# V stores of 8 or 16 tokens per segment, reordered by token and then segment, and without the number that the kernel's own scheduler held for them

## The chip, the cores and the metric

One core of one Trainium2 chip. The metric is the device time of the whole program in microseconds (us), the median of several runs. A run's granted clock is the mean share of full speed that TensorE was given; every run here had 0.989 to 1.000, and none was put in the slow state. Comparisons of kernels are ratios: the mean time of one kernel's runs over that of the other's runs of the same rounds on the same chip, so not quite the ratio of the medians that are quoted beside them.

## The reference

A memory-augmented attention layer and a gated feed-forward (FFN), both twice, on 2048 tokens of width 512. Attention runs over 64 segments of 32 tokens; 8 memory tokens, which are the output of the segment before, are put in front of each.

```python
for s in range(n_seg):
    h = jnp.concatenate([mem, xs], axis=1)          # 8 memory tokens + 32 tokens
    q, k, v = (einsum('btd,dhe->bhte', h, W) for W in (Wq, Wk, Wv))   # 32 heads of 128
    p = softmax(where(mask, einsum('bhqe,bhke->bhqk', q, k) * scale, -1e9))
    o = einsum('bhte,hed->btd', einsum('bhqk,bhke->bhqe', p, v), Wo)
    mem = o[:, :8]; outs.append(o[:, 8:])
...
x = x + A(layernorm(x)); x = x + B(layernorm(x))    # twice
```

The V rows of these 32 tokens don't depend on the memory. The kernel computes those of 24 of them ahead of time, for whole blocks of 4 segments, and parks them in HBM.

## The kernel before

`take_v` copies the normalised, transposed tokens of a block (4 segments, `BLK`) into columns of a weight tile of 128 columns; 24 tokens per segment fill 96 columns, and the last 32 are filled with 8 tokens per segment of another block (a "fill"). `v_pass` multiplies the tile with Wv in 8 column blocks of 512, copies each result to a staging tile and stores it to the HBM scratch `scr`, whose rows run by segment, then token.

```python
def take_v(self, pst, B, j, tile, keys, c0, r0, n):
    off = r0 + (MEM if j else 0)
    dst = fview(tile[:, 0, c0:c0 + 1], [(P, self.DC), (n, BLK), (1, n)])
    self.pl.add(("ACT", "DVE"), copy_ns(16 * n, True),
                lambda: (dst, fview(pst()[:, 0, off:off + 1], [(P, self.DC), (SEG, BLK), (1, n)])), r=[B], w=keys)

def v_pass(self, tile, keys, pieces, boot=False):
    ...                       # cut: matmuls and the copy to the staging tile vs
    for c0, j, b, r0, n in pieces:
        d = self.scr[j][b * BLK * XS:(b + 1) * BLK * XS, ps].rearrange("(i r) e -> i r e", i=BLK)[:, r0:r0 + n, :]
        tk = pl.add(("SP", "POOL") if boot else "SP", ..., lambda ...: ("dma", d, vs[c0:c0 + BLK * n, 0:512 * w]), ...)
        if n == 8:
            tk.land = 8000.0
```

Nothing is issued there. Every operation is a task with an expected duration; a list scheduler (`Planner`) plays the whole program through on a model of the engines, up to 24 rounds, keeps the round with the shortest model time, and the program is then written in that order. `land` is how long the model lets an SP transfer hold one of eight lanes:

```python
        if e == "SP":
            lanes.append(end + tk.land)          # 3000 ns unless set
            if len(lanes) >= 8:
                free[e] = max(end, lanes[-8])
```

## Time and profile before

| | before |
|---|---|
| time, median of 3 runs | 1872.28 us (1869.12 to 1873.32) |
| TensorE (PE) busy | 1822.6 us, 97% |
| chain that ended last | PE 92%, DMA 0% |
| 96 KB V stores (full blocks, 128 of them) | 16 semaphore updates, 1.82 us from issue to landing (median) |
| 32 KB V stores (fills, 96 of them) | 5 semaphore updates, 2.12 us |

The prediction below shows the lines. Landing times of SP transfers are not on the page; here and below they are counted from the updates of a transfer's semaphore in the trace.

### The profile page before, as it was taken

Reading aid. Unit: us, or ns where it says so; the run is one execution under the profiler, and the core shown is the slowest. Engines: PE = TensorE matmul, PEld = TensorE weight load, DVE = VectorE, ACT = ScalarE, POOL = GpSimd, SP = SyncE. Lnnn points to the kernel's source line nnn. Section 1 sums busy time; section 2 is a strip of 40 time slices with the busy share of each in tenths; the row PEclk is TensorE's granted clock in tenths of the full one; section 3 lists DMA queues with packets and bytes.
Section 4 is the critical chain, followed back from the end, with each engine's and each line's share of the span. In section 5 each row is a group of like instructions: output and inputs, shape, how many; then the busy total and the mean of one; then the engine's idle time right before and its main releaser. Section 6 shows DMA issues by size and latency. Waiting matters only on the chain.

```text
span 1869.7 us, 94235 instructions
## 1 busy us (share of the span) xinstructions
PE 1822.6 (97%) x41068; PEld 1577.4 (84%) x41282; DVE 1282.3 (69%) x4167; ACT 1137.3 (61%) x2692; POOL 583.2 (31%) x832
## 2 busy tenths in 40 slices
PE   7999999999999999999999999999999999999999
PEld 3578788888989898989988898989889898988787
DVE  5366577776777667776677677666777677766565
ACT  4655556666666666566666666666666666666554
POOL 5412012332423232333323233233323232333323
PEclk9999999999999999999999999999999999999999
DMA  9733334554645544555545554555545454455534
GB/s 354 247 102 103 89 86 119 153 155 129 182 124 153 151 143 124 151 151 149 166 128 152 147 143 131 141 152 153 157 121 152 136 156 122 141 152 145 158 100 138
DMA packets 130060, 273.83 MB, mean 146 GB/s; under 512 B 29254, under 2 KB 60750, under 8 KB 129646
## 3 DMA queue, kind: packets, MB, share of 16 engines
q0 software_dynamic: 59984, 184.49, 33.7%
q1 hardware_dynamic: 69662, 83.30, 15.5%
q8 instruction: 323, 5.29, 1.2%
q14 instruction: 91, 0.75, 0.1%
HBM read 221.85 MB, written 27.26 MB: 133 GB/s over the span
## 4 chain that ended last, share of the span: by engine, by line
PE 92%; DVE 4%; ACT 2%; issue 1%; DMA 0%; POOL 0%; SPq 0%; ACTq 0%; DVEq 0%; POOLq 0%
PE bank L708 32%; PE bank L811 16%; PE bank L910 11%; PE bank L570 9%; PE bank L680 7%; PE bank L722 5%; PE bank L781 4%; PE bank L794 4%; PE bank L934 4%; PE bank L540 1%; DVE st L735 1%; ACT otsb L1002 1%; DVE pb L764 0%; DMA vsb<-sst 0%; PE bank L878 0%
## 5 line engine op out<-in xcount | busy, mean ns | idle before, releaser
L708 PE MATMUL bank<-hT,wq_sb 128*128 128x80 bf16 (+1 forms) x8960 | 624.2, 198 | 5.7 <-issue 1.7
L708 PE MATMUL bank<-hT,wk_sb 128*128 128x80 bf16 (+1 forms) x8960 | 622.9, 198 | 1.4 <-issue 1.4
L1002 ACT CAST qku<-bank 128x480 bf16<-128x480 f32 (+3 forms) x770 | 393.9, 512 | 265.5 <-PE bank L708 253.3
L708 PEld LDWEIGHTS <-wq_sb 128*128 128x128 bf16 x8960 | 458.1, 99 | 27.9 <-issue 8.5
L708 PEld LDWEIGHTS <-wk_sb 128*128 128x128 bf16 x8960 | 450.7, 99 | 1.6 <-issue 1.6
L735 DVE TENSOR_TENSOR st<-bank,maskb 80x240 f32<-80x240 f32 (+1 forms) x732 | 268.7, 368 | 234.5 <-PE bank L722 227.7
L811 PE MATMUL bank<-otsb,wo_sb 128*128 128x80 bf16 (+1 forms) x8960 | 371.8, 198 | 7.4 <-ACT otsb L1002 5.5
L811 PEld LDWEIGHTS <-wo_sb 128*128 128x128 bf16 x8960 | 339.7, 99 | 21.5 <-issue 10.3
L902 POOL DMA_DIRECT2D wg<-in_B_w_gate_dram x217 | 165.0, 760 | 489.4 <-PE bank L910 419.7
L1002 ACT CAST otsb<-bank 128x480 bf16<-128x480 f32 (+3 forms) x420 | 200.8, 486 | 76.7 <-PE bank L794 61.9
L928 POOL DMA_DIRECT2D wd<-in_B_w_down_dram x217 | 153.7, 710 | 256.6 <-PE bank L794 98.5
L764 DVE TENSOR_TENSOR pb<-st,rz 80x480 bf16<-80x480 f32 x348 | 205.8, 592 | 3.5
L745 ACT ACTIVATE st<-st 80x240 f32<-80x240 f32 (+3 forms) x420 | 159.8, 382 | 64.6 <-DVE st L742 62.7
L1002 ACT CAST ptsb<-bank 128x480 bf16<-128x480 f32 (+3 forms) x315 | 155.3, 499 | 65.2 <-PE bank L781 62.9
L530 POOL TENSOR_TENSOR lns<-lns,negh 128x1 f32<-128x1 f32 (+1 forms) x79 | 45.4, 576 | 449.0 <-DVE lns L529 334.7
L722 PE MATMUL bank<-qku 128*80 128x80 bf16 (+1 forms) x2240 | 176.7, 202 | 1.8 <-ACT qku L1002 0.4
L747 DVE TENSOR_REDUCE sm<-st 80x6 f32<-80x240 f32 (+3 forms) x420 | 151.7, 362 | 35.5 <-ACT st L745 33.4
L910 PE MATMUL bank<-xnT,wg 128*128 128x128 bf16 (+2 forms) x1784 | 171.8, 219 | 1.5 <-ACT xnT L1002 0.2
L910 PE MATMUL bank<-xnT,wu 128*128 128x128 bf16 (+2 forms) x1784 | 171.2, 218 | 0.1
L722 PEld LDWEIGHTS <-qku 128*80 128x80 bf16 (+1 forms) x2240 | 129.9, 117 | 46.2 <-issue 11.5
L903 POOL DMA_DIRECT2D wu<-in_B_w_up_dram x217 | 162.5, 749 | 4.6 <-PE bank L781 1.4
L742 DVE TENSOR_TENSOR st<-st,mx 80x240 f32<-80x240 f32 (+3 forms) x420 | 155.7, 371 | 3.9
(98 smaller groups left out, 2475.1 us busy)
## 6 DMA issues: line engine op xcount, KB each, us to landing
wg<-in_B_w_gate_dram POOLq DMA_DIRECT2D x220, 256.0 KB, 4.3
wu<-in_B_w_up_dram POOLq DMA_DIRECT2D x220, 256.0 KB, 4.7
wd<-in_B_w_down_dram POOLq DMA_DIRECT2D x220, 256.0 KB, 5.2
vsb<-scr SPq DMA_DIRECT2D x508, 48.0 KB
vsb<-sst SPq DMA_DIRECT2D x280, 64.0 KB
scr<-vst SPq DMA_DIRECT2D x128, 96.0 KB
wv_sb<-in_A_Wv_dram SPq DMA_DIRECT2D x4, 1024.0 KB
wq_sb<-in_A_Wq_dram SPq DMA_DIRECT2D x5, 768.0 KB
```

Of the source, the lines that this page charges most:

```text
L570: nc.tensor.matmul(B[:, :], lhsT=tile[:, c, :], rhs=self.wv[:, c, cs], start=(c == 0), stop=(c == DC - 1))
L708: nc.tensor.matmul(o_ap, lhsT=W[:, c, h * P:(h + 1) * P], rhs=mv(c), start=(c == 0), stop=(c == DC - 1))
L722: nc.tensor.matmul(s_all(SB)[pr, uh - h0 + i, :], lhsT=qku[:, i, 0, 0:ncol], rhs=qku[:, i, 1, 0:ncol], start=True, stop=True)
L735: pl.add("DVE", dve_ns(n, True), lambda gsz=gsz, hs=hs, st=st, SB=SB, pj_=pj_, npj_=npj_, mk=mk, idx=idx: nc.vector.tensor_tensor(out=st[p ...
L742: pl.add("DVE", dve_ns(n), lambda gsz=gsz, hs=hs, st=st, mx=mx: nc.vector.tensor_tensor(out=st[pr, hs], in0=st[pr, hs], in1=mx[pr, hs].uns ...
L745: pl.add("ACT", act_ns(n), lambda hs=hs, st=st: nc.scalar.activation(out=st[pr, hs], in_=st[pr, hs], func=ACTF.Exp, scale=self.scale), r=s ...
L764: nc.vector.tensor_tensor(out=o, in0=st[pr, hs].unsqueeze(1).to_broadcast([npart, 2, gsz, L]), in1=rz[pr, :, 0:gsz].unsqueeze(3).to_broadc ...
L811: nc.tensor.matmul(WB[:, c * ncol:(c + 1) * ncol], lhsT=self.wo[:, h, c * P:(c + 1) * P], rhs=otsb[:, hl, 0:ncol], start=(h == 0 and c == ...
L902: pl.add("POOL", 760, lambda wg=wg, fs=fs: nc.gpsimd.dma_start(out=wg[:], in_=self.wgv[:, :, fs]), r=[("wo", self.H - 1)], w=[gk] + bt, la ...
L903: pl.add("POOL", 760, lambda wu=wu, fs=fs: nc.gpsimd.dma_start(out=wu[:], in_=self.wuv[:, :, fs]), r=[("wo", self.H - 1)], w=[uk] + bt, la ...
L910: nc.tensor.matmul(gu[:, 2 * i + k, 0:n], lhsT=W[:, c, i * P:(i + 1) * P], rhs=xnT[:, c, rw], start=(c == 0), stop=(c == DC - 1))
L1002: nc.scalar.copy(out=dst, in_=src)
```

## The change

The intent: the outermost dimension of these stores is 4; ordered by token and then segment it is 8 or 16, and such a store was expected to land sooner. With the slow store gone, the line that tells the scheduler of it goes too. Stores of 24 tokens per segment, which are contiguous, stay as they are.

```diff
-        dst = fview(tile[:, 0, c0:c0 + 1], [(P, self.DC), (n, BLK), (1, n)])
+        dst = fview(tile[:, 0, c0:c0 + 1], [(P, self.DC)] + ([(n, BLK), (1, n)] if n == XS else [(1, BLK), (BLK, n)]))
 ...
-                d = self.scr[j][b * BLK * XS:(b + 1) * BLK * XS, ps].rearrange("(i r) e -> i r e", i=BLK)[:, r0:r0 + n, :]
-                tk = pl.add(("SP", "POOL") if boot else "SP", ...
+                d = self.scr[j][b * BLK * XS:(b + 1) * BLK * XS, ps]
+                if n < XS:
+                    d = d.rearrange("(i r) e -> r i e", i=BLK)[r0:r0 + n]
+                pl.add(("SP", "POOL") if boot else "SP", ...
 ...
-                if n == 8:
-                    tk.land = 8000.0
```

So the edit has four parts that can be taken apart: the fills' stores, the stores of the start, the copies that now write with a stride, and the number.

More of the change, by code (lines that the diff above doesn't have):

```diff
@@ L580, in v_pass @@
             for c0, j, b, r0, n in pieces:
-                d = self.scr[j][b * BLK * XS:(b + 1) * BLK * XS, ps].rearrange("(i r) e -> i r e", i=BLK)[:, r0:r0 + n, :]
-                tk = pl.add(("SP", "POOL") if boot else "SP", {"SP": 450, "POOL": 760} if boot else 450,
+                d = self.scr[j][b * BLK * XS:(b + 1) * BLK * XS, ps]
+                if n < XS:
+                    d = d.rearrange("(i r) e -> r i e", i=BLK)[r0:r0 + n]
+                pl.add(("SP", "POOL") if boot else "SP", {"SP": 450, "POOL": 760} if boot else 450,
                        lambda vs=vs, d=d, c0=c0, n=n: ("dma", d, vs[c0:c0 + BLK * n, 0:512 * w]), lat=3000.0 + 1500.0 * boot,
```

## The prediction

> **What bounds the kernel now.** I read the page from the top: first the busy shares, then the chain that ended last.
>
> ```profile
> PE 1822.6 (97%) x41068; PEld 1577.4 (84%) x41282; DVE 1282.3 (69%) x4167; ACT 1137.3 (61%) x2692; POOL 583.2 (31%) x832
> ...
> q0 software_dynamic: 59984, 184.49, 33.7%
> q1 hardware_dynamic: 69662, 83.30, 15.5%
> ...
> PE 92%; DVE 4%; ACT 2%; issue 1%; DMA 0%; POOL 0%; SPq 0%; ACTq 0%; DVEq 0%; POOLq 0%
> ```
>
> TensorE (PE) is busy 1822.6 of 1869.7 us, so it is idle for 47.1 us in all. The weight loads cover 84%. The queue in which the V stores run after the start, q1 (the one that SyncE, SP, issues to), takes 15.5% of the DMA engines' time. The chain is PE for 92% and DMA for 0%. The kernel is bound by TensorE; a transfer counts only where TensorE stands still for it.
>
> Next the waits of PE, which say what its idle time was spent on, and of its weight loads:
>
> ```profile
> PE bank L513 <- DVE ident L451: 6.4, 1, 6.4
> PE bank L811 <- ACT otsb L1002: 5.5, 19, 0.7
> PE bank L540 <- DVE xn L531: 4.8, 5, 2.8
> PE bank L708 <- issue: 3.1, 5, 1.1
> PE bank L781 <- DVE pb L764: 2.3, 6, 1.0
> PE bank L794 <- DMA vsb<-sst: 1.5, 3, 0.9
> ```
>
> Columns are total us, times, longest. One row names a DMA: 1.5 us, for vsb<-sst, not for the stores at issue. From windows of 20 us I see where the rest lies: 0 to 20 us holds 10.7 us of idle (20.00 less 9.28), the last 9.7 us hold 3.2, 120 to 260 us hold 7.7; from 440 us on most windows have PE busy 19.6 to 19.9 of 20.
>
> Then the stores. The profile lists them as scr<-vst, 128 of 96 KB and 96 of 32 KB:
>
> ```profile
> scr<-vst SPq DMA_DIRECT2D x128, 96.0 KB
> ...
> scr<-vst SPq DMA_DIRECT2D x96, 32.0 KB
> ```
>
> The 96 small ones are the 8-token pieces ("fill" pieces: 4 fills x 3 pieces x 8 column blocks), all between 208 and 1379 us. Pieces of 16 tokens exist only in the start (before about 130 us), issued mostly from GpSimd (POOL). The waits of SP's queue and the view of the tile vst show who depends on them:
>
> ```profile
> SPq L668 <- PE bank L794: 441.9, 206, 6.6
> SPq L689 <- DVE sst L1004: 386.9, 55, 13.0
> ...
> SPq L668 <- DMA scr<-vst: 21.3, 18, 2.7
> ```
>
> ```profile
> who waited for it (us, times):
>   DVE st L735: 0.7, 1
> ```
>
> SP's queue waits 21.3 us in 18 places for a V store to land. It waits twenty times as long for TensorE (441.9 us for buffers that PV matmuls read), so it normally has slack. Of all engines only VectorE ever waited on the staging tiles vst, 0.7 us.
>
> **The size of the cost, from the trace's semaphore updates.** For each SP DMA I took the updates of its semaphore from issue to the next use of that semaphore. The 32 KB stores show 5 updates, the 96 KB ones 16, the 24-row loads vsb<-scr 13. Median time from issue to the last update: 2.12 us for 32 KB, 1.82 us for 96 KB. Issuing itself took 0.62 us against 0.31 us. Less issue, that is 1.50 against 1.51 us: the small store is slow in its issue[...]. 76 of the 96 landed within 2.45 us; 20 took 3 to 6.8 us, in the second half of a pass[...]. Their excess over 2.12 us sums to 49 us.
>
> [...]
>
> **The change part by part.**
>
> 1. Store shape. [...] What of it reaches TensorE: at most the row of 1.5 us and the matching row of weight loads (0.8 us). 0 to -2 us.
>
> 2. Boot stores. 24 pieces of 8 tokens and 24 of 16, nearly all from GpSimd, where 16 updates were seen for every shape and landing took 5 to 7 us whatever the shape (96-row ones too: 5.9 us). TensorE is busy 19.73 us of 20 in 20 to 80 us. 0 to -1 us.
>
> 3. The copies take_v. 24 of them now write 2-byte elements 8 bytes apart. On ScalarE the copies run at 0.83 ns an element (128, 256, 384 elements: 265, 376, 480 ns), a rate that should not care. On VectorE 225, 292, 358 ns is 0.52 ns an element; strided it might fall to 1.04, by my choice of the worst case, so 67 ns more for 128 elements. Three copies sat there. Under 0.5 us, and not on the chain.
>
> 4. The removed line `tk.land = 8000`. This is the part that can move something. The order of all instructions comes from a list scheduler in the kernel's build, and this number is how long it thinks an 8-token store holds one of SP's eight lanes. The trace's 2.12 us says that 3000 is the truer number. Did it matter in the plan? In 205.7 to 228.7 us SP issued 31 DMAs: 1.35 per us. Eight lanes at 3 us carry 2.7 per us. With a quarter of them at 8 us the mean is 4.25 us and they carry 1.9 per us; near the limit only in bursts. So in the old plan SP was sometimes held in a fill pass; in the new one it isn't, stores and loads move by some us, and from there the greedy choices and the best of 24 rounds may differ all the way down. The amount of work stays the same: same matmuls, same copies. What can differ is TensorE's idle time outside start and end, about 33 us (47.1 - 10.7 - 3.2), and slack within busy time. I take a change of a quarter of that either way, 8 us, as the typical size.
>
> Sum: direct -1 (0 to -3), plan 0 with a spread of 8. 1872.3 - 1 is about 1871; I lean slightly lower, since a truer model should on average not hurt: 1870.
>
> **The rivals.**
>
> - The slow stores were really holding back the loads behind them, and the V passes get faster as a whole. For it: the chain of waits passes once through scr<-vst near 211 us (1.69 us) and through vsb<-sst near 214.5 us (2.10 us), and fill passes at 200 to 220 us show PE busy only 18.03 of 20. Against: that stretch's idle is named DVE pb and ACT otsb as well, and DMA waits of PE add up to 2.3 us in the whole run. Even if every one of 12 fill passes gained 1 us: 1860.
> - The new order is worse: the plan was tuned with 8000, and the freed SP queue may bring vsb<-scr loads or stores earlier, against the FFN weight loads (queue q0, 33.7%), or put softmax work in a worse order. Speaking for it: 8% of the chain, some 150 us, runs through other engines. Against: all PE waits on such work are under 1 us but for three or so. It would make 1878 to 1885.
> - The transfers are hidden anyway and the plan hardly moves: 1870 to 1874, within the spread of the three runs (1869.12 to 1873.32). I think this the likeliest.
> - Strided writes or the new DRAM order slow the copies or the store: each run stays 1 KB (2 KB in the start), so no smaller pieces; copies are hidden. 0 to +2.
>
> **Range and chances.** Noise is 4 us from lowest to highest run; the plan's spread of 8 dominates. 8 in 10: 1861 to 1880. Over 2% is 37 us either way. Faster by that would need most of TensorE's 47 us idle gone, of which 14 lie at start and end: 2%. Slower by that needs nearly double the idle: 2%. Within: 96%.
>
> **What would show it.** In the changed trace: 32 KB stores with 9 updates[...], landing near 2.0 us with issue still about 0.6; fewer beyond 3 us; PE's busy time within 10 us of 1822.6 and its share of the chain at 90% or more; SP's wait for scr<-vst below 21.3 us without a gain in span; 96 KB stores unchanged at 1.8. The prediction is wrong if PE's idle time outside start and end moves by over 15 us: then the plan, not the stores, is the cause, and restoring the 8000 would tell.

Step 1's 0 to -2 us comes from the measured waits of 1.5 and 0.8 us of TensorE and its weight loads, and the sum came to -1 us on 1872.3, about 1871, put at 1870.

## More of the kernel before

One more line of the kernel before is needed for comparison: the busy times in one stretch, 200 to 1400 us, where all 96 fills lie. Its columns are the stretch, its length, then busy us and instructions of PE, of the weight loads (PEld), of VectorE (DVE), ScalarE (ACT) and GpSimd (POOL), and last the granted clock, the DMA share and GB/s.

```profile
200.00:1400.00 1200.00, 1178.06 (x26518) 1043.82 (x26658) 852.70 (x2779) 750.29 (x1719) 360.62 (x501) 1.00 0.49 140
```

PE shows 21.9 us of idle in these 1200 us.

## The result

The changed kernel took 1873.01 us (median of 4 runs, 1870.35 to 1873.84) beside 1872.53 us: ratio 1.0004, 95% interval 0.9986 to 1.0021. A second measurement on one chip with experiments gave 0.9992 (0.9978 to 1.0005). The predicted 1870 (1861 to 1880) holds it.

The stretch of 200 to 1400 us of the changed kernel:

```profile
200.00:1400.00 1200.00, 1184.69 (x26740) 1051.32 (x26868) 866.16 (x2788) 760.57 (x1734) 366.55 (x501) 1.00 0.49 140
```

PE's idle fell from 21.9 to 15.3 us there. But the whole time did not fall, so it came back elsewhere. The waits of PE (total us, times, longest) name one candidate; SP's wait for the V stores comes after them:

```profile
PE bank L540 <- DVE xn L531: 5.9, 6, 2.8
PE bank L795 <- DMA vsb<-sst: 3.0, 5, 1.3
PE bank L812 <- ACT otsb L1003: 1.9, 5, 0.5
```

```profile
SPq L669 <- DMA scr<-vst: 17.4, 18, 2.7
```

The wait for ScalarE's otsb fell from 5.5 to 1.9 us, that for xn (the normalised tokens) rose from 4.8 to 5.9. SP's wait for the V stores fell from 21.3 to 17.4 us. The fill stores show 9 semaphore updates and land in 1.93 us instead of 2.12, 6 of 96 over 3 us instead of 20; their issue takes 0.66 us instead of 0.62. Two of these signs were foretold, but are not the new shape's doing. Of the fill stores of e1 below (new shape, number kept) 27 took over 3 us, of those of e2 (old shape, number removed) none in one trace and 1 in the other: the late ones went with the number. And SP's wait is 21.3 us in one trace of e2 and 18.1 in the other, so a fall from 21.3 to 17.4 says little. Last, the copies. The groups of instructions of ScalarE, with shapes kept apart, before and then after:

```profile
L1002 ACT COPY xvl<-bank 128x128 bf16<-128x128 bf16 x12 | 2.6, 298 | 0.0
...
L1002 ACT COPY xvf<-bank 128x256 bf16<-128x256 bf16 x5 | 1.7, 376 | 0.9 <-PE bank L570 0.9
L1002 ACT COPY xvf<-bank 128x128 bf16<-128x128 bf16 x4 | 1.1, 265 | 1.4 <-PE bank L570 1.4
```

```profile
L1003 ACT COPY xvl<-bank 128x128 bf16<-128x128 bf16 x12 | 4.3, 542 | 0.0
L1003 ACT COPY xvf<-bank 128x256 bf16<-128x256 bf16 x5 | 3.3, 772 | 0.8 <-PE bank L571 0.8
...
L1003 ACT COPY xvf<-bank 128x128 bf16<-128x128 bf16 x4 | 1.8, 442 | 1.7 <-PE bank L571 1.7
```

The number after the comma is the mean in ns: 256 elements per partition went from 376 to 772, 128 from 265 to 442. The time between the two sizes is now 330 ns for 128 elements, 2.6 ns each, where it was 0.87.

To see where time is lost I used the moment at which each of the 41,282 weight loads starts, which all traces have in full. The changed kernel is 1.0 us behind at load 250 (43 us), 1.4 at load 750, 1.4 at load 3500 (190 us), 4.7 at load 3750 (200 us), and then gains: 1.2 at load 9000, -3.4 at load 36,500. So something delays the start, and something else pays it back.

### The profile page after: what moved, and what is told of

The parts are those of the page before. It is cut to its first block, busy times and chain, and to the rows that moved or that the text cites. A ratio compares the mean times of both kernels' runs of the same rounds, so it can differ in the third digit from the quotient of the medians.

```text
span 1868.6 us, 94264 instructions
## 1 busy us (share of the span) xinstructions
PE 1824.7 (98%) x41085; PEld 1579.3 (85%) x41282; DVE 1294.5 (69%) x4168; ACT 1143.7 (61%) x2691; POOL 586.3 (31%) x832
## 4 chain that ended last, share of the span: by engine, by line
PE 92%; DVE 4%; ACT 2%; issue 1%; DMA 1%; SPq 0%; POOL 0%; ACTq 0%; DVEq 0%
PE bank L709 32%; PE bank L812 16%; PE bank L911 11%; PE bank L571 9%; PE bank L681 7%; PE bank L723 5%; PE bank L935 4%; PE bank L782 4%; PE bank L795 4%; PE bank L540 1%; DVE pb L765 1%; ACT otsb L1003 1%; DVE st L736 0%; DVE lns L527 0%; DVE sm L748 0%
## 5 line engine op out<-in xcount | busy, mean ns | idle before, releaser
L812 PE MATMUL bank<-otsb,wo_sb 128*128 128x80 bf16 (+1 forms) x8960 | 375.8, 198 | 4.1 <-ACT otsb L1003 1.9
L530 POOL TENSOR_TENSOR lns<-lns,negh 128x1 f32<-128x1 f32 (+1 forms) x79 | 51.1, 648 | 502.3 <-DVE lns L529 445.3
L1003 ACT CAST ptsb<-bank 128x480 bf16<-128x480 f32 (+3 forms) x300 | 147.6, 501 | 55.5 <-PE bank L782 54.1
```

Source lines behind the costliest of these rows:

```text
L812: nc.tensor.matmul(WB[:, c * ncol:(c + 1) * ncol], lhsT=self.wo[:, h, c * P:(c + 1) * P], rhs=otsb[:, hl, 0:ncol], start=(h == 0 and c == ...
L1003: nc.scalar.copy(out=dst, in_=src)
```

## The experiments

The theory that I took from this: the stores themselves are hidden; the new plan gains several us; the strided copies and something about the start take them back. The rival: the plan does nothing much, and the gain is what the new stores bring. The experiments run through the parts. In each I compared the instruction order: with 8000 kept, TensorE's order is that of the kernel before, instruction for instruction; with 8000 removed it is that of the changed kernel. All results were reported correct, that of e8 too: see there.

A summary first. "Clock loss" is (1 - granted clock) x span, the mean over a kernel's runs. It is measured (the record rounds the clock to 0.001, which is 1.9 us), but that taking it off gives the time at full clock is an assumption, good where TensorE is the bound.

| kernel | 8000? | stores in the start | fills' stores | copies | ratio to before (95%) | mean us | clock loss us | mean less loss |
|---|---|---|---|---|---|---|---|---|
| before | yes | old | old | plain | 1 | 1873.8, 1872.5, 1872.7 | 5.4, 4.6, 4.9 | 1868.4, 1867.9, 1867.8 |
| after | no | new | new | strided writes | 1.0004, 0.9992 | 1872.6, 1871.0 | 10.3, 8.7 | 1862.3, 1862.3 |
| e1 shape only | yes | new | new | strided writes | 1.0028 (1.0015 to 1.004) | 1879.2 | 7.9 | 1871.4 |
| e5 | yes | new | new | strided reads | 1.0012 (0.9998 to 1.0025) | 1876.4 | 8.2 | 1868.2 |
| e2 number only | no | old | old | plain | 0.9959 (0.9945 to 0.9973), 0.9955 (0.9941 to 0.997) | 1866.3, 1864.3 | 6.3, 5.2 | 1860.0, 1859.1 |
| e3 | no | old | new | strided in fills | 0.9964 (0.9952 to 0.9977) | 1867.4 | 8.2 | 1859.2 |
| e7 | no | new | new | strided reads | 0.9981 (0.9967 to 0.9995) | 1869.0 | 8.4 | 1860.6 |
| e9 | no | new | old | strided reads in the start | 0.9978 (0.9964 to 0.9992) | 1868.5 | 8.2 | 1860.3 |
| e8 copies only | no | old | old | strided writes | 0.9971 (0.9955 to 0.9987) | 1867.6 | 5.9 | 1861.7 |
| e4 stores doubled | yes | old | 192 halves | plain | 1.0001 (0.9989 to 1.0014) | 1872.8 | 4.9 | 1867.9 |

### The two halves of the edit: e1 and e2

e1 is the changed kernel with the number put back; e2 is the kernel before with the number removed.

```diff
 # e1, against after                 # e2, against before
+                if n == 8:          -                if n == 8:
+                    tk.land = 8000.0  -                    tk.land = 8000.0
```

> New store shape and new copies, but the number 8000 kept: TensorE's instruction order is then the same as in the kernel before, instruction for instruction. Theory (transfers are hidden; the store's shape costs nothing that TensorE sees, the slower strided copies cost about 1 us in the start): 1872 to 1875, ratio 0.9995 to 1.002; 32 KB stores with 9 updates landing at 1.93 us instead of 2.12. Rival (slow stores held the V passes back): 1860 to 1868.

> Old store shape and old copies, only the line with 8000 removed: TensorE's order is that of the changed kernel. Theory: the plan alone gains the 2 to 4 us that the changed kernel makes up between 440 and 1860 us, and the start isn't slowed by copies, so 1868 to 1872, ratio 0.997 to 1.000. Rival (the plan does nothing, the shape does it all): equal to before within 0.05%, 1872.5. Stores with 5 updates, landing about 2.12 us.

Measured: e1 1878.92 us (ratio 1.0028), e2 1865.12 us (0.9959; in a repeat 1863.53, 0.9955). Two effects of opposite sign: removing the number gains 8 us, the new shape costs 5 us under the old plan. e1 was slower than I expected, e2 faster. The rival falls on both counts: the stores do not gain (e1 is slower than before, although its stores land in 1.94 us) and the plan is the gain.

> The changed kernel itself, once more, beside the kernel before on one chip. If plan (-0.41% alone) and shape (+0.28% alone) add up, the ratio is near 0.9987, between 0.9970 and 1.0004; if the shape costs more under the new plan, it stays at 1.0004 or above.

The changed kernel again: 0.9992, inside the range of the sum, 0.9987. The halves add up within the noise.

> The land-only kernel once more. Ratio near 0.9959 again, 0.9945 to 0.9975. Also a test of the clock: kernels with the old store shape lost 5.2 us a run to a granted clock below 1 (30 runs, (1 - clock) x span), those with the new shape 8.5 us (36 runs). If that goes with the store shape, this one loses 4 to 6.5; if it goes with the plan, 8 to 10.

The repeat held, ratio and clock loss both (5.2 us).

### The stores made worse: e4

The kernel before, its order kept, each small store issued as two of half the width, which doubles their number, their issue time and the lanes they take.

```diff
+                if ... tk.land == 8000.0 and tk.on == "SP":
+                    for q in range(2):
+                        nc.sync.dma_start(out=got[1][:, :, 256 * q:256 * q + 256], in_=got[2][:, 256 * q:256 * q + 256])
```

> The kernel before with its order kept, each of the 96 small stores issued as two of half the width: [...]0.6 us more of SP's queue each, 8 stores more per pass. Theory (stores are hidden): ratio 1.000, within 0.002, with SP's waits for scr<-vst grown to 30 us or more. Rival (slow fill stores cost what the change set out to gain): each pass loses 1 us or more, ratio 1.006 or above.

The transfers of e4, and SP's wait for them (total us, times, longest):

```profile
scr<-vst SPq DMA_DIRECT2D x128, 96.0 KB
scr<-vst SPq DMA_DIRECT2D x192, 16.0 KB
```

```profile
SPq L668 <- DMA scr<-vst: 11.5, 18, 1.8
```

Ratio 1.0001, interval 0.9989 to 1.0014: doubling these stores costs nothing that these runs can tell (0.14% at most). My side expectation failed: SP's wait for the stores did not grow to 30 us but fell to 11.5, the half stores landing in 1.88 us instead of 2.12. So fill stores are hidden in the kernel before, with room to spare, and an earlier landing could hardly gain anything; e3 below tests the new shape itself.

### The copies: e5, e7 and e8

e5 is e1 with the copies walked the other way, tokens outside and segments inside. The same elements go to the same places, but the writes are contiguous and the reads from PSUM take the stride (64 bytes).

```diff
-  dst: [(P, DC), (1, BLK), (BLK, n)]      src: [(P, DC), (SEG, BLK), (1, n)]
+  dst: [(P, DC), (BLK, n), (1, BLK)]      src: [(P, DC), (1, n), (SEG, BLK)]
```

> As e1 (number 8000 kept, new store shape), but the copies walk tokens outside and segments inside: they write contiguously and read PSUM with a stride of 64 bytes. If the slow part was the write of 2-byte elements 8 bytes apart, ScalarE's 256-element copy returns from 0.772 to about 0.38 us and the start's delay of 1 us is gone: 1871 to 1873. If any strided side costs the same, it stays at 0.7 to 0.8 us and the time equals e1's.

The same groups of ScalarE in e5:

```profile
L1005 ACT COPY xvl<-bank 128x128 bf16<-128x128 bf16 x12 | 2.6, 298 | 0.0
...
L1005 ACT COPY xvf<-bank 128x256 bf16<-128x256 bf16 x5 | 1.7, 375 | 0.9 <-PE bank L571 0.9
```

The slow thing was the strided write: with the stride on the reading side 256 elements are back at 375 ns. VectorE keeps part of the cost, 425 ns for 256 where the plain copy took 292 and the strided write 722. The delay at load 250 is gone (0.0 us against 0.9 in e1), and e5's mean is 2.8 us below e1's. The mean less the clock loss, 1868.2, is that of the kernel before. The time itself, 1876.21, was above my 1871 to 1873; e5 shares with e1 a delay near 190 us, for which see below.

e8 goes the other way: the strided copies and nothing else of the shape, under the new plan. The rows are permuted.

```diff
 # against e2
-        dst = fview(tile[:, 0, c0:c0 + 1], [(P, self.DC), (n, BLK), (1, n)])
+        dst = fview(tile[:, 0, c0:c0 + 1], [(P, self.DC)] + ([(n, BLK), (1, n)] if n == XS else [(1, BLK), (BLK, n)]))
```

> The land-only kernel with the strided copies and nothing else; the stores keep the old order, so the rows come out permuted and the result is wrong on purpose. Theory (the strided copies are all that the new shape costs in work): 2 us over the land-only kernel, ratio 0.9968 to 0.998. Rival (the stores carry the cost): equal to the land-only kernel, and the clock loss stays at 5 to 6.

It was reported correct all the same, presumably because the exchange of some V rows moves the outputs by less than the tolerance; so the check against the reference would not have caught a mistake in the permutation. That copy and store use the same order in the other kernels is read from the code alone. The time is what counts here: 1867.02 us, 0.9971, a mean of 3.3 us above e2 (2.6 less the clock loss). By load 600 (76 us) it was 1.5 us behind, in steps at 15, 41 and 74 us, where the copies of the start lie; where the rest arises was not traced.

e7 is the changed kernel with the copies of e5.

> The changed kernel (new store shape, 8000 removed), but with copies that write contiguously and read with the stride. Theory (of the shape only the strided copies cost time[...]): equal to the land-only kernel, ratio 0.9959 to 0.997; the 250th weight load at 43.2 us as before, not 44.2. Rival[...]: 0.998 to 1.000.

1869.03 us, 0.9981: 2.0 us of mean below the changed kernel, but not at e2's 0.996 as expected; it lies in the range of the rival, by which the stores cost time too. Not at load 250, where it is level, but near 190 us it loses 1.6 us. So the stores of the shape do cost something, in one place.

### The stores in the start: e3 and e9

e3 is the changed kernel with old stores and plain copies in the start; only the fills are new.

```diff
 # cut: take_v gets boot, and with it copies as before
+                if n < XS and boot:
+                    d = d.rearrange("(i r) e -> i r e", i=BLK)[:, r0:r0 + n, :]
```

> The changed kernel, but in the start (GpSimd's stores) the old order and the contiguous copies; the 96 fill stores keep the new shape. Theory (strided copies delay the start by 1.0 to 1.5 us, nothing else in the start matters): 1 to 1.5 us faster than the changed kernel, 1871.5, with copies of 256 elements on ScalarE back at 0.376 us from 0.772. Rival (the start's delay is the plan's): same time as the changed kernel and the same delay of 1 us at the 250th weight load.

1867.42 us, 0.9964, near e2's 0.9959: the fills' new stores neither gain nor cost, within the 2 to 3 us of the intervals. Along the weight loads e3 stays within 1 us of e2's first trace from load 4600 to 39,900. The changed kernel keeps its distance from that trace too, 4.5 us at load 4000 (218 us) and 5.2 at load 36,500, so nearly all of it comes up before the fills. (e2's own two traces are 1.9 us apart at load 4000.) By the ratios to before (0.9964 against 0.9992 and 1.0004) it was 5 to 7 us faster than the changed kernel, not 1 to 1.5.

e9 is the reverse: new stores in the start with the copies of e5, fills as before.

```diff
 # cut: the copies of the start as in e5, those of the fills as before
+                if n < XS and not boot:
+                    d = d.rearrange("(i r) e -> i r e", i=BLK)[:, r0:r0 + n, :]
```

> New plan; new store shape in the start alone, with copies that write contiguously; the 96 fill stores keep the old shape. Theory (neither store shape matters): equal to the land-only kernel, 0.995 to 0.9975. If the start's new stores raise the clock loss, it is near 8 us and the ratio 0.998; if the fills' do, it is near 5 and the ratio 0.996.

1868.68 us, 0.9978, a mean of 4.3 us above e2 (1.3 less the clock loss). My theory, that neither store shape matters, falls here for the start. The trace shows the place. GpSimd issues the FFN weights; the two views are its instructions in order of time (start us, us, what; in brackets the idle time before and what ended it), first of e2's repeat, then of e9:

```profile
182.96 0.75 POOL L901 DMA_DIRECT2D wu<-in_B_w_up_dram  x1
184.57 0.75 POOL L900 DMA_DIRECT2D wg<-in_B_w_gate_dram  x1 [0.86 <-PE bank L908]
```

```profile
185.63 0.75 POOL L906 DMA_DIRECT2D wu<-in_B_w_up_dram  x1
189.24 0.76 POOL L905 DMA_DIRECT2D wg<-in_B_w_gate_dram  x1 [2.86 <-PE bank L913]
```

The second wg is GpSimd's 89th transfer. It waits for an update of TensorE's semaphore. In e2 it starts 0.06 us after that update. In e9 the update comes at 187.18 and the start at 189.24, 2.06 us after it, with GpSimd idle. In every trace of a kernel with new stores in the start this transfer is 2.06 us late (e9, e7, e5, e1, the changed kernel, and the plan with 5000), in those with old ones 0.06 (before, both of e2, e3, e4, e8, the plan with 12000). In three pairs of the same plan (e2's repeat and e9, e3 and e7, before and e5) I compared every transfer of GpSimd that TensorE released: this is the only one that came a microsecond or more later. Behind it stands the layernorm's power on GpSimd, then xn on VectorE, then TensorE:

```profile
191.16 0.40 PE L540 MATMUL bank<-ident,xn 128*128 128x128 bf16 x4 [0.20 <-DVE xn L531]
```

That is e2's repeat, 0.2 us of wait for xn; the waits of PE in this place are 1.8 us in e9, e7, the changed kernel and the plan with 5000, 1.2 us in e1 and e5. In e9 (total us, times, longest):

```profile
PE bank L540 <- DVE xn L531: 1.8, 1, 1.8
```

So the new stores of the start cost some 1.6 us of TensorE here.

That comparison looked for late transfers only. Taken both ways, the traces show that the stop isn't the new stores' own. Under both plans GpSimd stops at about every 30th transfer, with old stores too, mostly for 0.5 to 0.8 us. With 8000 removed and old stores in the start it does so at the 76th (1.4 us), 106th, 135th, 165th, 224th and so on to the end; with new stores at the 89th (2.0 us), 119th, 149th, 178th, 266th and so on (some steps of the series don't show). So the shape of the start's stores shifts a series that both shapes have, and with the new ones its first and longest stop falls where TensorE waits behind it. What makes the stops isn't shown. One thing differs ahead of them: by 127 us the kernel before had made 3,168 packets of 8 bytes in this queue, the changed one 366.

### The number: 5000 and 12000

Two other numbers, no other edit: the changed kernel with 5000, and the kernel before with 12000.

> The changed kernel with 5000 in place of 8000 or the default 3000: another plan, no other edit. Theory (the number only picks one of many orders, and the time moves by some us either way): 1864 to 1880 and no trend with the number. Rival (a truer number gives a better plan): between the times of 8000 (1879, shape only) and 3000 (1873).

> The kernel before with 12000 in place of 8000: a fourth plan, no other edit. If a truer number gives a better plan (3000 is best, 8000 worse), this is as slow as before or slower, 1.000 to 1.006; if the number only picks an order, anywhere between 0.995 and 1.005.

5000 with the new shape: 1872.09 us, ratio 0.9998. 12000 with the old shape: 1941.45 us, ratio 1.0368 (1.0348 to 1.0388), far outside what I expected. Taking the clock loss off, with the new shape 8000, 5000 and 3000 give 1871.4, 1864.3 and 1862.3; with the old shape 12000, 8000 and 3000 give 1927.0, 1868 and 1859.5. From 5000 up the time rises with the number in both rows. Between 3000 and 5000 no difference is shown: the means are 1871.0 and 1872.2 us, with intervals that overlap. The small stores of all these kernels land in 2.12 us or less (medians).

The stretch of 200 to 1400 us with 12000, then with the number removed (e2's repeat):

```profile
200.00:1400.00 1200.00, 1141.53 (x25176) 1001.52 (x25301) 818.44 (x2661) 709.70 (x1597) 341.82 (x475) 0.99 0.47 133
```

```profile
200.00:1400.00 1200.00, 1185.18 (x26750) 1052.23 (x26879) 864.04 (x2784) 758.98 (x1736) 369.95 (x507) 1.00 0.50 142
```

PE's idle in it is 58.5 us with 12000, 21.9 with 8000, 14.8 with 3000. The kernel with 12000 is 1.2 us behind the kernel before at load 3750 (200 us), 71.8 behind at load 31,500 (1446 us in the kernel before), and 71.2 at load 39,000. So all but some 4 of the 74 us that it loses by the end fall into the time of the fills, on average some 6 us for each of the 12 passes. What TensorE waits for in the whole run with 12000:

```profile
PE bank L811 <- ACT otsb L1002: 13.5, 40, 1.2
PE bank L910 <- DMA wu<-in_B_w_up_dram: 12.5, 17, 2.4
PE bank L540 <- DVE xn L531: 10.8, 14, 2.8
```

Not the stores, but work and weight loads that stand in a worse order. The loss is in the plan. I read it so: the order was made for an SP queue that the model held back for long and the chip did not; that the number alone does it is shown, by which choices of the scheduler is not. Nor do a few numbers exclude that some of these plans came out well or badly by chance.

A caution on idle times: traces of most of these kernels lack some 200 of the 41,282 matmul records (41,068 before), which count as idle. Four traces have all of them: e4 with the order of before, e7 and the second trace of the changed kernel with that of after, and the plan with 5000. Their PE busy times in this stretch are 1186.71, 1191.70, 1191.13 and 1192.94 us. The gain of the plan there is then 4.4 to 5.0 us, not the 6.6 of the two incomplete traces, and 5000 does no worse there than 3000.

### The clock

Every trace has two to five periods of 3.4, 6.8 or 10.2 us in which the granted clock is one half, that with 12000 ten; the last is cut short by the end of the run. The columns are as above; the stretch holds the wait for xn, in before and then in after:

```profile
193.00:201.00 8.00, 7.52 (x209) 7.52 (x209) 3.81 (x12) 5.02 (x12) 0.00 (x0) 1.00 0.21 66
```

```profile
193.00:201.00 8.00, 5.38 (x107) 5.07 (x104) 1.09 (x4) 2.31 (x7) 2.10 (x4) 0.79 0.57 181
```

In the changed kernel half the clock was taken for 3.4 us from 196.4 us on, shortly after TensorE had waited for xn. TensorE did not stand still all that time: in the 3.4 us before this it was still busy for 1.15 us, and no wait there was longer than 1.8 us; ahead of the period at 142 us in the kernel before, it was busy for 3.28 of 3.4 us. Over all runs before the last call, kernels with a new store anywhere lost 8.5 us to the clock (36 runs, standard deviation 2.1), those without 5.2 (30 runs, 2.5). e9 lost 8.2, e2 5.2 and e8 5.9, as that would have it. But e3, with the old stores in the start and no wait at 190 us, lost 8.2 as well, and the slow plan with 12000 lost 14.6 with old stores. Low activity came just before some of the periods and not before others, so what brings them on, and why the new shape has more of them, in the fills as well as in the start, isn't settled.

## Why the prediction was right, and where its steps were not

The time fell into the range, 3 us from the centre. That was luck in part: terms that I had mis-sized cancelled.

- **Bound by TensorE, stores hidden (right for the fills).** Busy 1824.7 us after, 2.1 more; 92% of the chain. e4 shows the hiding directly.
- **Step 1, store shape, "0 to -2 us" (size off at the lower end).** 9 updates as foretold, landing 1.93 us against "near 2.0", issue 0.66 against "about 0.6". The part after the issue fell from 1.49 to 1.26 us, by 0.23, and the issue grew by 0.04. So the store was slow after its issue too, not in its issue alone. TensorE gained nothing: e3 is not faster than e2 (0.9964 against 0.9959).
- **Step 2, boot stores, "0 to -1 us" (wrong sign).** They cost about 1.6 us of waits, because a stop of GpSimd falls in a bad place, and perhaps clock; e9's mean is 4.3 us above e2's.
- **Step 3, copies, "under 0.5 us, and not on the chain" (wrong).** The premise that ScalarE's rate "should not care", which no trace had shown, failed: 2.6 ns an element, three times the plain copy's. VectorE's worst case was 1.04 ns; it measured 2.2, (722 - 444) / 128. And the copies of the start stand ahead of TensorE's first matmuls. In all the strided copies cost 3.3 us in e8, of which 1.5 by 76 us; e1 less e5 gives 2.8, the changed kernel less e7 2.0.
- **Step 4, the number, "plan 0 with a spread of 8" (the direction was called a slight lean, the size was wrong).** It is -8 us, and +69 us for 12000. I treated the plan as a lottery; from 5000 up it has a trend, and the measured landing of 2.1 us, which I had in hand, said which way. (A count in this step is off too: from 205.7 to 228.7 us SP issued 33 transfers, 1.4 per us, not 31.)
- **The clock** was not in the sum: 3.5 to 5 us more loss for the changed kernel.

As means against before: plan -8, copies +3.3, stores of the start +4.3 (clock included), fills 0 to 1, in all about 0; measured +0.7 and -1.5 (ratios 1.0004 and 0.9992). The rival "hidden anyway" named the cause for the fills; "the new order is worse" had the wrong sign.

The faster version that comes out is e2: remove the number and leave the stores alone, 0.9955 to 0.9959 of the kernel before.

## What to carry to other kernels

Take an edit apart before believing that it does nothing: here a gain of 8 us and a loss of equal size gave a ratio of 1.000. Where a kernel is ordered by a model, measure the constants in the trace first, because a landing time set at 8 us for 2.1 cost 8 us against one of 3, and one at 12 another 69; 2.1 itself was not tried. When a layout is turned for the sake of a transfer that nobody waits for, look at which compute instruction pays for it, and turn the side that reads, which cost ScalarE nothing here (375 ns for 256 elements against 376 of the plain copy; the strided write 772) and VectorE less than the write (425 ns against 722; plain 292).
